# Attention and two MLPs on one core: transposes of P in float32r, row sums on DVE, PV halves joined by SBUF DMAs, and a new order of steps

## The chip, the cores and the metric

The kernel runs on one core of a Trainium2 chip. The metric is the device time of one execution in microseconds (us), as the median of the timed runs; lower is better. The engines are PE (TensorE; PEld is its loading of weights), DVE (VectorE), ACT (ScalarE), POOL (GpSimd) and SP (SyncE, which here only issues DMAs).

## The reference

Three stages follow each other. Attention takes q, k and v of shape (2, 8, 1152, 64), averages neighbouring rows of q (1152 becomes 576), and computes softmax(q k^T / 8) v. Its result, laid out as 1152 tokens by 512, goes through two MLPs.

```python
q_pool = q.reshape(B, H, S // 2, 2, D).mean(axis=3)
scores = scale * np.matmul(q_pool, k.transpose(0, 1, 3, 2))
attn = np.exp(scores - scores.max(-1)); attn /= attn.sum(-1) + 1e-9
x = heads_side_by_side(attn @ v)              # 1152 x 512
h = np.maximum(x @ w_in, 0); x = (s * h * h + b) @ w_out      # d_ff 2048
return ((x @ w_a) * (x @ w_b)) @ w_out2                       # d_ff 1536
```

## The kernel before

Matmuls run in float32r, and where more exactness is wanted an operand is split into a high and a low half (names ending in h and l): ACT makes the high half by a copy with a cast, DVE the low half by a subtraction.

Attention is worked in eight pairs of heads (NP, n from 0 to 7). A pair has nine blocks of 128 query rows (ORDER, i from 0 to 8; the block in the middle, number 4, holds the last 64 rows of both heads). The global number of a block is g = 9n + i. A block goes through these steps, each a short function that the list STEPS names:

- S01 and S2: scores on PE, 768 columns into one of two PSUM tiles and 384 into one of four shared PSUM banks (s_mm01, s_mm2). M01, M2, C: row maxima on DVE. X2, X01: exponentials on ACT into an SBUF tile E, with the row sums as a by-product, read by two small instructions.
- A: POOL adds the two row sums (s_add, L453). R: DVE takes the reciprocal (L457). N: POOL multiplies E by it (L464). E has three rooms.
- Ta, Tb, Tc: nine 128x128 transposes of E on PE, by the float32 identity, into shared banks (p_tr, L481: four, four and one). ha, hb, hc (ACT, L493) and La, Lb, Lc (DVE, L499) read each bank once and write the halves of P transposed, p2 and p3. A bank is free again when its last reader is done (bank, bank_read).
- PP: behind Tc three transposes of the next pair's k (float32r, L349) or q (float32, L369) ride in the same bank; EVh and EVl read them out.
- P0 to P3: the PV matmuls (pv_mm, L515): for each head and each of two column groups (256 and 320 columns), V against p2 or p3. V stands as high and low halves side by side, so that the 128 rows of the result are two halves that must be added.
- PVc and PVd: ACT copies the one half of 64 rows to SBUF onto the partitions of the other (pv_copy, L524), and DVE adds the other half from PSUM (pv_add, L534). XS: POOL splits the sum into xa_h and xa_l, the input of the first MLP (x_split, L95 and L98); for the last pair ACT and DVE do that.
- KS, VS, QP: POOL splits k and v and pools q, and then SP issues the load of the next pair. CV steps convert the first MLP's weights.

The order of all steps is written out by hand in SCHED, one text for one pair; a mark ' behind a name says that the step belongs to the pair before (two marks: two before), a comma to the next one. Each engine works its own part of that order strictly in sequence. MM, Fa, Fd and Fp are pieces of the first MLP that run in the last pair's order.

After attention come the first MLP (weights converted from 64-bit words along the way), the second MLP, which forms its products by sums of blocks with tiles u1, u2, u3 and u5 (u_tile, L884; copy_up and add_up write and read them), and the output.

Of the kernel before, what the change touches and what calls it, by code (L numbers as in the profile page):

```python
# [27 lines left out]
PP.8' Lb.7' Tb.8' R.0 EVh.8' hc.8' hb.8' N.0 Fp.0''''''''''''''' P2.5' M01.2 P2.6' Lc.8' S2.2 P2.7' P2.8' Ta.8'
Lb.8' M2.2 Tb.0 X01.1 C.2 A.1 R.1 S01.3 PVc.2' ha.8' PVd.2' Ta.0 La.8' hb.0 X2.2 X01.2 Tc.0 PP.0 S2.3 MM.0' N.1
Lb.0 Tc.1 M01.3 PP.1 EVh.0 A.2 M2.3 hc.0 XS.0' S01.4 ha.0 Lc.0 C.3 S2.4 R.2 EVh.1 hc.1 La.0 X2.3 CV.2 CV.3 EVl.1  # L30
N.2 X01.3 Ta.1 Lc.1 ha.1 A.3 CV.4 Tb.1 hb.1 M01.4 P3.0' P3.1' M2.4 S01.5 La.1 CV.0, C.4 R.3 P3.2' P3.3' KS.0,
CV.6' Lb.1 X2.4 Ta.2 P3.4' Tb.2 Tc.2 ha.2 P3.5' PP.2 M01.5 hb.2 P3.6' N.3 CV.5 La.2 Lb.2 CV.7' QP.0, CV.1, X01.4
CV.8''''''''''''''''''''''''''''''''''''''''''''''''''''''''''' A.4 hc.2 P3.7' S2.5 EVh.2 M2.5 P3.8' VS.1 Tb.3
Lc.2 S01.6 PVc.3' C.5 Fa.0' P0.0 PVd.3' P0.1 Fd.0' hb.3 R.4 X2.5 X01.5 P0.2 Ta.3 Lb.3 S2.6 N.4 M01.6 Tc.3 M2.6
PP.3 P0.3 ha.3 P0.4 S01.7 C.6 P0.5 EVh.3 La.3 hc.3 MM.1''''''''''''''''''''''''''''''''''''''''''''''' P0.6 Lc.3
P0.7 M01.7 X2.6 S2.7 X01.6 P0.8 A.5 XS.1' PVc.0 M2.7 Ta.4 R.5 PVd.0 C.7 ha.4 A.6 Tb.4 Tc.4 R.6 hb.4 PP.4 N.5
S01.8 La.4 Ta.5 EVh.4 N.6 hc.4 Lb.4 X2.7 Tc.5 PP.5 Lc.4 ha.5 QP.1, P1.0 P1.1 M01.8 La.5 S2.8 EVh.5 P1.2 M2.8
hc.5 X01.7 Tb.5 EVl.5 hb.5 A.7 C.8 R.7 Lc.5 P1.3
# [1077 lines left out]
```

## Time and profile before

| | |
|---|---|
| three timed runs, median (lowest to highest) | 686.64 us (686.63 to 687.0) |
| profiled execution, from its first to its last instruction | span 684.6 us, 11850 instructions |
| busy, share of the span: PE | 674.3 us, 98% |
| PEld | 647.0 us, 95% |
| DVE | 521.9 us, 76% |
| ACT | 400.3 us, 58% |
| POOL | 366.6 us, 54% |
| granted TensorE clock, mean | 1.000 |
| first attention scores to the last PV matmul | from about 8 us to 274 us |

The profile is one execution of its own. It gives no time outside of its span; the median of the timed runs is 2.0 us above the span. Matmul ends are modelled and overlap, so that the distance from one start to the next tells what a matmul costs in a row of matmuls, and its printed duration does not. The same holds, to a smaller degree, for DVE and ACT, whose next instruction often starts before the end of the one before. Idle time of an engine is put down to the one whose signal came last.

### The profile page before, as it was taken

To read this page: it belongs to the slowest core of one execution; us is meant where nothing else is said; L and a number is where in the kernel's file an instruction comes from. 1 tells how busy PE (TensorE), PEld (TensorE's weight loads), DVE (VectorE), ACT (ScalarE), POOL (GpSimd) and SP (SyncE) were. 2 spreads that over 40 slices of the span, in tenths; PEclk is the share of its full clock that TensorE was granted. 3 is DMA by queue.
4 is the path that set the end of the run, shared out by engine and by line. 5 is a ranking of instruction groups with operands and counts; after the bars stand their busy time and mean duration, and the time that the engine had idled before them with its cause. 6 is when DMAs were issued, how large, how long until landed. Compare 5 with 4: busy or idle time off the path is not lost.

```text
span 684.6 us, 11850 instructions
## 1 busy us (share of the span) xinstructions
PE 674.3 (98%) x4446; PEld 647.0 (95%) x4446; DVE 521.9 (76%) x963; ACT 400.3 (58%) x869; POOL 366.6 (54%) x374
## 2 busy tenths in 40 slices
PE   8999999999999999999999999999999999999997
PEld 7899999999999998999999999999999999998885
DVE  6999999999999996584545744879987888886431
ACT  6998999999999986454531421435433434444321
POOL 5879797979788883586535535510225442430000
PEclk9999999999999999999999999999999999999999
DMA  7121121303030010423223232250132323134004
GB/s 232 38 70 62 44 70 35 82 25 105 2 105 16 20 65 1 152 94 123 63 72 113 63 103 83 64 182 1 62 117 69 125 62 123 62 90 157 0 1 138
DMA packets 25914, 52.93 MB, mean 77 GB/s; under 512 B 1665, under 2 KB 2689, under 8 KB 25857
## 3 DMA queue, kind: packets, MB, share of 16 engines
q1 hardware_dynamic: 25776, 52.04, 23.7%
q8 instruction: 35, 0.57, 0.4%
q14 instruction: 23, 0.18, 0.1%
q10 hardware_dynamic: 80, 0.13, 0.1%
HBM read 49.81 MB, written 2.36 MB: 76 GB/s over the span
## 4 chain that ended last, share of the span: by engine, by line
PE 84%; DVE 9%; ACT 3%; POOL 2%; issue 1%; DMA 1%; SPq 0%; ACTq 0%; POOLq 0%; DVEq 0%
PE ps L630 28%; PE pp L630 17%; PE pp L950 11%; PE pv L515 9%; PE t L481 7%; PE s L404 6%; PE s L411 3%; DVE p3l L499 2%; DVE sm L430 1%; ACT p3h L493 1%; PE t L349 1%; PE t L369 1%; DVE xs L534 1%; DVE sm L427 1%; ACT x L354 1%
## 5 line engine op out<-in xcount | busy, mean ns | idle before, releaser
L481 PE MATMUL t<-ident,e 128*128 128x128 f32 x648 | 98.9, 276 | 2.3 <-POOL e L464 1.0
L464 POOL TENSOR_SCALAR e<-e,sm 128x1152 f32<-128x1152 f32 (+1 forms) x73 | 89.8, 1232 | 10.6 <-DVE sm L457 7.1
L481 PEld LDWEIGHTS t<-ident,e 128*128 128x128 f32 x648 | 75.3, 140 | 12.9 <-POOL e L464 2.3
L965 POOL TENSOR_TENSOR ab<-ab,at 128x576 f32<-128x576 f32 x24 | 35.0, 1478 | 91.0 <-ACT ab L960 87.2
L764 POOL TENSOR_SCALAR r<-r,sb_s,sb_b 128x384 f32<-128x384 f32 (+1 forms) x46 | 41.0, 902 | 57.7 <-DVE r L761 57.7
L499 DVE TENSOR_TENSOR p3l<-t,p3h 128x512 fp32r<-128x512 f32 (+1 forms) x120 | 64.2, 554 | 6.6 <-ACT p3h L493 4.2
L427 DVE TENSOR_REDUCE sm<-s 128x1 f32<-128x768 f32 x72 | 68.2, 948 | 0.1
L446 ACT ACTIVATE e<-s,sm 128x768 f32<-128x768 f32 x72 | 66.5, 923 | 0.4 <-DVE sm L435 0.4
L493 ACT CAST p3h<-t 128x512 fp32r<-128x512 f32 (+1 forms) x120 | 56.2, 485 | 5.1 <-PE t L481 2.7
L758 ACT ACTIVATE r<-ps 128x384 f32<-128x384 f32 (+1 forms) x46 | 20.1, 505 | 61.8 <-PE ps L630 61.7
L761 DVE SCALAR_TENSOR_TENSOR r<-ps,r 128x384 f32<-128x384 f32 (+1 forms) x46 | 23.8, 567 | 37.2 <-ACT r L758 37.2
L499 DVE TENSOR_TENSOR p2l<-t,p2h 128x512 fp32r<-128x512 f32 x96 | 50.8, 549 | 0.9 <-ACT p2h L493 0.7
L142 ACT ACTIVATE f<-raw 128x1024 f32<-128x1024 f32 x34 | 38.8, 1140 | 17.9 <-issue 11.1
L515 PE MATMUL pv<-p3h,v 128*128 128x320 f32 x144 | 47.6, 338 | 0.4 <-DVE p2l L499 0.4
L493 ACT CAST p2h<-t 128x512 fp32r<-128x512 f32 x96 | 45.0, 501 | 5.1 <-PE t L481 4.3
L439 ACT ACTIVATE e<-s,sm 128x384 f32<-128x384 f32 x72 | 43.0, 597 | 5.8 <-DVE sm L457 4.7
L630 PE MATMUL ps<-xa_h,wh 128*128 128x384 f32 (+1 forms) x200 | 45.3, 330 | 0.1
L146 DVE SCALAR_TENSOR_TENSOR f<-raw,f 128x1024 int32<-128x1024 int32 x34 | 44.5, 1309 | 1.1
L630 PE MATMUL ps<-xa_h,wl 128*128 128x384 f32 (+1 forms) x200 | 45.0, 328 | 0.0
L630 PE MATMUL ps<-xa_l,wh 128*128 128x384 f32 (+1 forms) x200 | 45.0, 328 | 0.0
L166 POOL TENSOR_TENSOR wl<-f,wh 128x1024 fp32r<-128x1024 f32 x16 | 40.5, 2531 | 7.1 <-ACT wh L198 5.9
L630 PE MATMUL ps<-gh,wh 128*128 128x384 f32 x192 | 43.7, 336 | 0.0
(142 smaller groups left out, 2047.1 us busy)
## 6 DMA issues: line engine op xcount, KB each, us to landing
raw<-in_moe_w_out_dram SPq DMA_DIRECT2D x14, 1024.0 KB, 5.0
raw<-in_moe_w_in_dram SPq DMA_DIRECT2D x8, 1024.0 KB, 5.7
raw<-in_moe_w_a_dram SPq DMA_DIRECT2D x6, 1024.0 KB, 5.2
raw<-in_moe_w_b_dram SPq DMA_DIRECT2D x6, 1024.0 KB, 5.1
vn<-in_v_dram SPq DMA_DIRECT2D x8, 576.0 KB, 4.0
kn<-in_k_dram SPq DMA_DIRECT2D x7, 576.0 KB, 3.9
qn<-in_q_dram SPq DMA_DIRECT2D x7, 512.0 KB, 3.8
out_dram<-ab SPq DMA_DIRECT2D x8, 256.0 KB, 2.6
```

The source lines that it names most:

```text
L146: nc.vector.scalar_tensor_tensor(out=f, in0=lo, scalar=29, in1=f, op0=ALU.logical_shift_right, op1=ALU.bitwise_or)
L404: nc.tensor.matmul(ps[:, c, 0:384], w, x[:, c * 384:(c + 1) * 384], start=(z == 0), stop=(z == len(pr) - 1))
L427: nc.vector.reduce_max(small(g)[:, 0:1], SPS[g, 0][:, :, 0:384], axis=AX.XY)
L439: nc.scalar.activation(out=e_tile(g)[:, 768:1152], in_=SPS.pop((g, 1))[:, 0:384], func=AF.Exp, bias=m[:, 2:3], accum_out=m[:, 3:4])
L446: nc.scalar.activation(out=e_tile(g)[:, 0:768].rearrange("p (a c) -> p a c", a=2), in_=SPS.pop((g, 0))[:, :, 0:384], func=AF.Exp, bias=m[: ...
L464: nc.gpsimd.tensor_scalar(out=e[:, c], in0=e[:, c], scalar1=m[:, 6:7], scalar2=1.0, op0=ALU.mult, op1=ALU.mult)
L481: nc.tensor.transpose(ps[:, i * 128:(i + 1) * 128], E[g][:, (c0 + i) * 128:(c0 + i + 1) * 128], ident)
L493: nc.scalar.copy(out=p_dst(g)[0][:, c0:c0 + n], in_=p_src(g, z))
L499: nc.vector.tensor_tensor(out=l, in0=p_src(g, z), in1=h.bitcast(F32), op=ALU.subtract)
L515: nc.tensor.matmul(ps[:, 0:N], V[n, hd][:, c].rearrange("p a d -> p (a d)"), p, start=(t == 0), stop=(t == 2 * NC - 1))
L630: nc.tensor.matmul(ps, a, c[:, o:o + n], start=(first and z == 0), stop=(last and z == 2), skip_group_check=more)
L950: nc.tensor.matmul(ps, a[x], w2_at[kf][c], start=(kf == 0 and y == 0), stop=(kf == KF2 - 1 and y == 2))
```

## The change

- E becomes one tensor of three rooms, e, and a second tensor, er, of type float32r is laid on the same bytes. The exponentials and N write by the name e. The transposes read by the name er, with the float32r identity, and write float32r into the bank. Since the two names are two tensors to the framework, three kinds of waits are written by hand: the first transpose of each group waits for N (E_DONE), and the first exponential that reuses a room waits for the transposes that read it (E_READ, e_written).
- A moves from POOL to DVE.
- For all pairs but the last, PVc copies all 128 rows of the bank, and that is the bank's only reader. PVd becomes one DMA from SBUF to SBUF, issued by SP, that moves 64 rows; for the second head a further DMA moves the other 64 rows beside the first head's. XS on POOL first adds the two tiles and then splits as before.
- A bank for a group's last transpose may be taken by the riding transposes first (t_bank), so PP may stand ahead of Tc.
- SCHED is written anew. The set of steps is the same. The block of steps that stood at the end of the text now stands at its beginning, one period later, QP.1 among them. One CV step runs four pairs earlier.
- The u tiles of the second MLP lie in the first two rooms of e instead of in a pool of their own.

```diff
--- before.py
+++ after.py
@@ -21,21 +21,21 @@
 
 
 SCHED = """
-S01.0 Ta.6' X2.8' Tb.6' Lb.5' N.7' Tc.6' PP.6' P1.4' M01.0 ha.6' hb.6' La.6' P1.5' P1.6' S2.0 EVh.6' P1.7' hc.6'
-Lb.6' X01.8' Lc.6' P1.8' M2.0 KS.1 Ta.7' EVl.6' S01.1 A.8' PVc.1' VS.0
-CV.9''''''''''''''''''''''''''''''''''''''''''''''''''''''''''''' R.8' C.0 ha.7' P2.0' PVd.1' P2.1' P2.2' X2.0
-Tc.7' La.7' PP.7' X01.0 hc.7' S2.1 Tb.7' N.8' M01.1 M2.1 A.0 C.1 EVh.7' hb.7' S01.2 Lc.7' P2.3' P2.4' X2.1 Tc.8'
-PP.8' Lb.7' Tb.8' R.0 EVh.8' hc.8' hb.8' N.0 Fp.0''''''''''''''' P2.5' M01.2 P2.6' Lc.8' S2.2 P2.7' P2.8' Ta.8'
-Lb.8' M2.2 Tb.0 X01.1 C.2 A.1 R.1 S01.3 PVc.2' ha.8' PVd.2' Ta.0 La.8' hb.0 X2.2 X01.2 Tc.0 PP.0 S2.3 MM.0' N.1
-Lb.0 Tc.1 M01.3 PP.1 EVh.0 A.2 M2.3 hc.0 XS.0' S01.4 ha.0 Lc.0 C.3 S2.4 R.2 EVh.1 hc.1 La.0 X2.3 CV.2 CV.3 EVl.1
-N.2 X01.3 Ta.1 Lc.1 ha.1 A.3 CV.4 Tb.1 hb.1 M01.4 P3.0' P3.1' M2.4 S01.5 La.1 CV.0, C.4 R.3 P3.2' P3.3' KS.0,
-CV.6' Lb.1 X2.4 Ta.2 P3.4' Tb.2 Tc.2 ha.2 P3.5' PP.2 M01.5 hb.2 P3.6' N.3 CV.5 La.2 Lb.2 CV.7' QP.0, CV.1, X01.4
-CV.8''''''''''''''''''''''''''''''''''''''''''''''''''''''''''' A.4 hc.2 P3.7' S2.5 EVh.2 M2.5 P3.8' VS.1 Tb.3
-Lc.2 S01.6 PVc.3' C.5 Fa.0' P0.0 PVd.3' P0.1 Fd.0' hb.3 R.4 X2.5 X01.5 P0.2 Ta.3 Lb.3 S2.6 N.4 M01.6 Tc.3 M2.6
-PP.3 P0.3 ha.3 P0.4 S01.7 C.6 P0.5 EVh.3 La.3 hc.3 MM.1''''''''''''''''''''''''''''''''''''''''''''''' P0.6 Lc.3
-P0.7 M01.7 X2.6 S2.7 X01.6 P0.8 A.5 XS.1' PVc.0 M2.7 Ta.4 R.5 PVd.0 C.7 ha.4 A.6 Tb.4 Tc.4 R.6 hb.4 PP.4 N.5
-S01.8 La.4 Ta.5 EVh.4 N.6 hc.4 Lb.4 X2.7 Tc.5 PP.5 Lc.4 ha.5 QP.1, P1.0 P1.1 M01.8 La.5 S2.8 EVh.5 P1.2 M2.8
-hc.5 X01.7 Tb.5 EVl.5 hb.5 A.7 C.8 R.7 Lc.5 P1.3
+M01.8' EVh.4' Lc.4' N.6' ha.5' P1.0' P1.1' P1.2' QP.1 EVh.5' La.5' EVl.5' X01.7' P1.3' hc.5' S2.8' Tb.5' M2.8' A.7'
+P1.4' S01.0 C.8' Lc.5' hb.5' X2.8' Ta.6' R.7' Lb.5' Tb.6' M01.0 ha.6' N.7' Tc.6' KS.1 PP.6' hb.6' P1.5' P1.6' La.6'
+X01.8' hc.6' Lb.6' CV.9''''''''''''''''''''''''''''''''''''''''''''''''''''''''''''' P1.7' S2.0 EVh.6' P1.8' A.8'
+Ta.7' M2.0 R.8' C.0 EVl.6' PVc.1' N.8' S01.1 Lc.6' ha.7' X2.0 X01.0 P2.0' PVd.1' P2.1' Tb.7' PP.7' Tc.7' La.7' VS.0
+S2.1 P2.2' M01.1 EVh.7' hc.7' P2.3' hb.7' S01.2 M2.1 Lc.7' C.1 Tc.8' A.0 PP.8' X2.1 Lb.7' EVh.8' P2.4' R.0
+Fp.0''''''''''''''' hc.8' M01.2 Tb.8' Lc.8' P2.5' S2.2 hb.8' Lb.8' P2.6' Ta.8' X01.1 M2.2 A.1 ha.8' N.0 C.2 P2.7' R.1
+P2.8' PVc.2' Tb.0 PVd.2' S01.3 hb.0 La.8' X2.2 Lb.0 CV.8'''''''''''''''''''''''''''''''''''''''''''''''''''''''''''
+N.1 S2.3 PP.1 M2.3 Ta.0 PP.0 X01.2 Tc.1 ha.0 M01.3 EVh.1 La.0 hc.1 Tc.0 EVh.0 C.3 KS.0, hc.0 MM.0' EVl.1 Lc.1 X2.3
+S01.4 S2.4 A.2 Ta.1 Lc.0 X01.3 Tb.1 R.2 ha.1 P3.0' M01.4 P3.1' M2.4 A.3 La.1 hb.1 Lb.1 CV.0, P3.2' S01.5 N.2 P3.3'
+Tb.2 R.3 C.4 hb.2 Ta.2 XS.0' P3.4' P3.5' ha.2 CV.3,,,, P3.6' N.3 M01.5 X2.4 Lb.2 P3.7' P3.8'
+MM.1''''''''''''''''''''''''''''''''''''''''''''''' La.2 X01.4 CV.6' CV.7' CV.2 S2.5 PP.2 Tc.2 PVc.3' CV.1, Tb.3 EVh.2
+M2.5 S01.6 P0.0 PVd.3' P0.1 hc.2 Lc.2 P0.2 S2.6 P0.3 C.5 hb.3 Lb.3 A.4 PP.3 X2.5 X01.5 Fd.0'''''' QP.0, Tc.3 Ta.3
+M01.6 EVh.3 P0.4 R.4 M2.6 hc.3 P0.5 ha.3 VS.1 Fa.0'' CV.4 S01.7 A.5 N.4 C.6 Lc.3 S2.7 R.5 X01.6 P0.6 P0.7 P0.8 La.3
+X2.6 Ta.4 M01.7 A.6 Tb.4 M2.7 PVc.0 R.6 ha.4 N.5 XS.1' CV.5 PVd.0 hb.4 Tc.4 C.7 PP.4 S01.8 La.4 X2.7 Ta.5 Lb.4 hc.4
+Tc.5 PP.5
 """.split()
 
 @with_exitstack
@@ -262,7 +262,12 @@
     ps_s01 = s01.enter_context(tc.tile_pool(name="ps_s01", bufs=2, space=PSUM))
     banks = [right(att, f"ps_{i}", 1, space=PSUM) for i in range(4)]
     v_p = right(att, "vv", 2)
-    e_p = right(att, "e", 3)
+    e_all = nc.alloc_sbuf_tensor("e", [128, 3, S], F32, side="right")
+
+
+    er_all = nc.alloc_sbuf_tensor_at("er", [128, 3, S], F32R, offset=nc.lookup_mloc(e_all).addr)
+    e_at = [e_all.ap()[:, i] for i in range(3)]
+    er_at = [er_all.ap()[:, i] for i in range(3)]
     pt_p = right(att, "pt", 1)
     xs_p = right(att, "xs", 2)
     sm_p = right(att, "sm", 4)
@@ -420,8 +425,14 @@
 
     def e_tile(g):
         if g not in E:
-            E[g] = e_p.tile([128, S], F32, tag="e", name="e")
+            E[g] = e_at[g % 3]
         return E[g]
+
+    E_DONE = {}
+
+    def e_written(g, ins):
+        for t in E_READ.pop(g - 3, ()):
+            after(ins, t, mybir.DependencyReason.ANTI)
 
     def s_max01(g):
         nc.vector.reduce_max(small(g)[:, 0:1], SPS[g, 0][:, :, 0:384], axis=AX.XY)
@@ -436,21 +447,23 @@
 
     def s_exp2(g):
         m = SM[g]
-        nc.scalar.activation(
+        ins = nc.scalar.activation(
             out=e_tile(g)[:, 768:1152], in_=SPS.pop((g, 1))[:, 0:384], func=AF.Exp, bias=m[:, 2:3], accum_out=m[:, 3:4]
         )
+        e_written(g, ins)
         bank_read(("s2", g))
 
     def s_exp01(g):
         m = SM[g]
-        nc.scalar.activation(
+        ins = nc.scalar.activation(
             out=e_tile(g)[:, 0:768].rearrange("p (a c) -> p a c", a=2), in_=SPS.pop((g, 0))[:, :, 0:384], func=AF.Exp,
             bias=m[:, 2:3], accum_out=m[:, 4:5],
         )
+        e_written(g, ins)
 
     def s_add(g):
         m = SM[g]
-        nc.gpsimd.tensor_scalar(out=m[:, 5:6], in0=m[:, 3:4], scalar1=1e-9, scalar2=m[:, 4:5], op0=ALU.add, op1=ALU.add)
+        nc.vector.tensor_scalar(out=m[:, 5:6], in0=m[:, 3:4], scalar1=1e-9, scalar2=m[:, 4:5], op0=ALU.add, op1=ALU.add)
 
     def s_rec(g):
         m = SM[g]
@@ -461,7 +474,9 @@
         e = E[g]
 
         for c in (slice(512, S), slice(0, 512)) if g == 0 else (slice(0, S),):
-            nc.gpsimd.tensor_scalar(out=e[:, c], in0=e[:, c], scalar1=m[:, 6:7], scalar2=1.0, op0=ALU.mult, op1=ALU.mult)
+            E_DONE[g, c.start] = nc.gpsimd.tensor_scalar(
+                out=e[:, c], in0=e[:, c], scalar1=m[:, 6:7], scalar2=1.0, op0=ALU.mult, op1=ALU.mult
+            )
 
     def p_dst(g):
         hd, j = ORDER[g % 9]
@@ -474,12 +489,19 @@
 
     PTC = ((0, 4), (4, 4), (8, 1))
 
+    def t_bank(g, z):
+        if (g, z) not in TP:
+            TP[g, z] = bank(("t", g, z), 2 * (g >= 0) + (rides(g) if z == 2 else 0))
+        return TP[g, z]
+
     def p_tr(g, z):
-        ps = bank(("t", g, z), 2 + (rides(g) if z == 2 else 0))
+        ps = t_bank(g, z)
         c0, n = PTC[z]
         for i in range(n):
-            nc.tensor.transpose(ps[:, i * 128:(i + 1) * 128], E[g][:, (c0 + i) * 128:(c0 + i + 1) * 128], ident)
-        TP[g, z] = ps
+            t = nc.tensor.transpose(ps[:, i * 128:(i + 1) * 128].bitcast(F32R), er_at[g % 3][:, (c0 + i) * 128:(c0 + i + 1) * 128], identr)
+            if i == 0:
+                after(t, E_DONE[g, 512 if g == 0 and z else 0], mybir.DependencyReason.DATA)
+        E_READ.setdefault(g, []).append(t)
 
     def p_src(g, z):
         c0, n = PTC[z]
@@ -499,6 +521,12 @@
         nc.vector.tensor_tensor(out=l, in0=p_src(g, z), in1=h.bitcast(F32), op=ALU.subtract)
         bank_read(("t", g, z))
 
+    SYNC = mybir.DependencyClass.Sync
+    E_READ = {}
+
+    def after(ins, earlier, why):
+        tc.add_manual_dep(ins.ins, earlier.ins.name, mybir.DependencyInfo(SYNC, why), reason="e and er are one room")
+
     TP = {}
     PV = {}
     XS = {}
@@ -507,7 +535,7 @@
         key = (n, hd, big_seg)
         N = 256 + NX if big_seg else 256
         if lo == 0:
-            PV[key] = bank(("pv", key), 2)
+            PV[key] = bank(("pv", key), 2 if n == NP - 1 else 1)
         ps = PV[key]
         for t in range(lo, hi):
             c, x = divmod(t, 2)
@@ -520,8 +548,11 @@
         ps = PV[n, hd, big_seg]
         N = 256 + NX if big_seg else 256
         a, o = (0, 64) if hd == 0 else (64, 0)
-        tmp = PVT[n, hd, big_seg] = xs_p.tile([128, 256 + NX], F32, tag="tmp", name="tmp")
-        nc.scalar.copy(out=tmp[a:a + 64, 0:N], in_=ps[o:o + 64, 0:N])
+        tmp = PVT[n, hd, big_seg] = xs_p.tile([128, 256 + NX], F32, tag=f"t{hd}", name="tmp")
+        if n == NP - 1:
+            nc.scalar.copy(out=tmp[a:a + 64, 0:N], in_=ps[o:o + 64, 0:N])
+        else:
+            nc.scalar.copy(out=tmp[:, 0:N], in_=ps[:, 0:N])
         bank_read(("pv", (n, hd, big_seg)))
 
     def pv_add(n, hd, big_seg):
@@ -529,14 +560,22 @@
         N = 256 + NX if big_seg else 256
         if (n, big_seg) not in XS:
             XS[n, big_seg] = xs_p.tile([128, 256 + NX], F32, tag="xs", name="xs")
-        xs, tmp = XS[n, big_seg], PVT.pop((n, hd, big_seg))
+        xs, tmp = XS[n, big_seg], PVT[n, hd, big_seg]
         a = 64 * hd
+        if n < NP - 1:
+
+            nc.sync.dma_start(out=xs[a:a + 64, 0:N], in_=tmp[64 - a:128 - a, 0:N])
+            if hd == 1:
+                nc.sync.dma_start(out=PVT[n, 0, big_seg][64:128, 0:N], in_=tmp[64:128, 0:N])
+            return
         nc.vector.tensor_tensor(out=xs[a:a + 64, 0:N], in0=ps[a:a + 64, 0:N], in1=tmp[a:a + 64, 0:N], op=ALU.add)
         bank_read(("pv", (n, hd, big_seg)))
 
     def x_split(n, big_seg):
         xs = XS.pop((n, big_seg))
         N = 256 + NX if big_seg else 256
+        if n < NP - 1:
+            nc.gpsimd.tensor_tensor(out=xs[:, 0:N], in0=xs[:, 0:N], in1=PVT[n, 0, big_seg][:, 0:N], op=ALU.add)
         b, hp = n // HP, n % HP
         c0 = b * SP + (256 if big_seg else 0)
         c = slice(c0, c0 + N)
@@ -565,8 +604,7 @@
     def ride(n, i):
         g = 9 * n + i
         if rides(g):
-            ps = TP[g, 2] if n >= 0 else bank(("t", g, 2), rides(g))
-            pend[n, i] = RIDES[i][2](n + RIDES[i][0], ps[:, 128:512])
+            pend[n, i] = RIDES[i][2](n + RIDES[i][0], t_bank(g, 2)[:, 128:512])
 
     def evac(n, i, z):
         if (n, i) in pend and pend[n, i][z]:
@@ -881,7 +919,8 @@
         U = {}
 
         def u_tile(name):
-            U[name] = u_p.tile([128, 2, HC], F32, tag=name, name=name)
+            i = ("u1", "u2", "u3", "u5").index(name)
+            U[name] = halves(e_at[i // 2][:, i % 2 * SP:(i % 2 + 1) * SP])
             return U[name]
 
         def copy_up(name, ps):
@@ -909,7 +948,6 @@
         ps_b.close()
         for i in range(4):
             ps2.append(ctx.enter_context(tc.tile_pool(name=f"pp{i}", bufs=1, space=PSUM, side=("right", "left")[i // 2])))
-        u_p = ctx.enter_context(tc.tile_pool(name="u", bufs=1))
         m2_p = ctx.enter_context(tc.tile_pool(name="m2", bufs=1))
         ab0 = m2_p.tile([128, 8, NT], F32, tag="ab", name="ab")
         ab1 = []
```

## Rows read from the trace of the kernel before

**Rows 1.** Busy us and instructions per engine, clock, DMA share, GB/s, three stretches.

```profile
47.82:80.14 32.32, 32.21 (x242) 31.02 (x241) 30.75 (x74) 29.82 (x80) 27.36 (x34) 1.00 0.19 56
...
240.00:260.00 20.00, 19.38 (x135) 17.68 (x133) 19.64 (x44) 17.19 (x45) 17.26 (x19) 1.00 0.17 54
...
300.00:320.00 20.00, 20.00 (x117) 20.00 (x116) 14.50 (x20) 10.34 (x20) 15.57 (x12) 1.00 0.19 65
```

**Rows 2.** Chain of waits: start us, length us, engine, tile, line.

```profile
47.82 1.43 PE s L404 x8
...
209.53 1.44 PE s L404 x8
...
268.40 3.20 PE ps L630 x24
```

**Rows 3.** Timeline of PE: start us, length us, line, out<-in, shapes.

```profile
113.76 0.33 PE L411 MATMUL s<-x,qm_h 128*128 128x384 f32 x1
...
114.46 1.04 PE L481 MATMUL t<-ident,e 128*128 128x128 f32 x8
...
115.48 0.30 PE L515 MATMUL pv<-p3l,v 128*128 128x320 f32 x1
...
115.92 0.51 PE L404 MATMUL s<-x,qh 128*128 128x384 f32 x2
...
121.56 0.28 PE L515 MATMUL pv<-p2l,v 128*128 128x256 f32 x1
121.68 0.28 PE L515 MATMUL pv<-p2h,v 128*128 128x256 f32 x1
```

**Rows 4.** Timeline of PE in narrow windows around one run of K transposes.

```profile
118.78 0.22 PE L349 MATMUL t<-identr,kc 128*128 128x128 f32 x1
...
118.90 0.25 PE L349 MATMUL t<-identr,kc 128*128 128x128 f32 x1
118.99 0.38 PE L515 MATMUL pv<-p3h,v 128*128 128x320 f32 x1
119.21 0.31 PE L515 MATMUL pv<-p3l,v 128*128 128x320 f32 x1
```

**Rows 5.** Timeline of DVE from 114.33 us on.

```profile
114.33 0.28 DVE L499 TENSOR_TENSOR p2l<-t,p2h 128x128 fp32r<-128x128 f32 x1
114.52 0.95 DVE L427 TENSOR_REDUCE sm<-s 128x1 f32<-128x768 f32 x1
115.39 0.55 DVE L430 TENSOR_REDUCE sm<-s 128x1 f32<-128x384 f32 x1
115.85 0.68 DVE L499 TENSOR_TENSOR p2l<-t,p2h 128x512 fp32r<-128x512 f32 x1
116.45 0.14 DVE L435 TENSOR_REDUCE sm<-sm 128x1 f32<-128x2 f32 x1
116.51 0.15 DVE L457 RECIPROCAL sm<-sm 128x1 f32<-128x1 f32 x1
116.58 0.67 DVE L499 TENSOR_TENSOR p2l<-t,p2h 128x512 fp32r<-128x512 f32 x1
```

**Rows 6.** Groups by line, five periods: count, busy us, mean ns, idle before.

```profile
L534 DVE TENSOR_TENSOR xs<-pv,tmp 64x320 f32<-64x320 f32 x10 | 4.8, 484 | 0.2
L534 DVE TENSOR_TENSOR xs<-pv,tmp 64x256 f32<-64x256 f32 x10 | 4.2, 422 | 0.2
```

**Rows 7.** Groups by line on POOL, the same five periods.

```profile
L453 POOL TENSOR_SCALAR sm<-sm 128x1 f32<-128x1 f32 x46 | 13.3, 289 | 15.7 <-ACT e L446 13.0
...
L98 POOL TENSOR_TENSOR xa_l<-xs,xa_h 128x320 fp32r<-128x320 f32 x5 | 4.4, 875 | 0.4
```

**Rows 8.** DMA issues of the page: count, KB each, us to landing.

```profile
raw<-in_moe_w_in_dram SPq DMA_DIRECT2D x8, 1024.0 KB, 5.7
...
qm<-in_q_dram SPq DMA_DIRECT2D x16, 32.0 KB, 3.2
```

## The prediction

> **What bounds the kernel now.** I read the busy time per stretch first, then the chain of waits, then the timeline of TensorE by starts, and the other engines after it. In a stretch of attention PE is busy 32.21 of 32.32 us, but DVE 30.75 and ACT 29.82 are close, and in the MLP stretch (300 to 320) PE is busy 20.00 of 20 with DVE at 14.50 [rows 1]. The chain names the same score matmul once per pair of heads, six times from 47.82 to 209.53: a period of 32.33 us [rows 2]. From 268.40 on it runs through the first MLP's matmuls, where PE has no idle time. So whatever attention saves should stand at the end.
>
> A busy PE is no proof that PE is the limit, so I count one period by starts. Scores: 8 blocks of 6 matmuls and one of 12 make 60, at (114.46 - 113.76)/4 = 0.175 us: 10.5. PV: 36 of 320 columns at (115.92 - 115.48)/3 = 0.147 and 36 of 256 at 0.12: 9.6. A run of 8 float32 transposes takes 115.48 - 114.46 - 0.147 = 0.873, its after-effect on the next matmul included: 0.109 each; 81 of P and 9 of q make 9.8 [rows 3]. The K transposes are float32r already: three start at 118.78, (118.84) and 118.90, PV follows at 118.99 and its second matmul at 119.21 instead of 0.147 later, so a run of three costs 0.283, and six make 1.7 [rows 4]. Sum 31.6 of 32.33. PE is the limit, with 0.7 lost.
>
> DVE by starts: M01 0.87, M2 0.46, C 0.06, R 0.07 for each of 9 blocks; 18 large L at 0.60, 9 small at 0.19; q's lower halves 1.5 (estimate from the same steps); four PV adds, some 1.6 by their durations less overlap [rows 5, 6]. Sum 13.1 + 10.8 + 1.7 + 1.5 + 1.6 = 28.7 to 29.2; I use 29.0. That is 5 to 6% under its busy time, because ends overlap. ACT's 29.82, less the same share, is an estimate of 28.2.
>
> **The transposes of P.** In float32r they have the K transposes' form (same shapes, same engine). Within a run the step is 0.06; the run's last one costs 0.09, and the next matmul is 0.075 late: 0.1 per run on top. The new order has 15 runs in a period; in two of them q's float32 transposes come last. So 99 x 0.062 = 6.1, plus 13 x 0.1 = 1.3, plus q's 1.0, is 8.4 against 11.5 now: 3.1 less. PE would need 28.5. Bounds per transpose: 0.06 below, and above the 0.109 of now. The nearest rows, K's, decide for 0.06.
>
> The longest float32r run now is three [rows 4]. The Trainium skill (TensorE: Matmul & The Clock Gate, "Back-to-back issue gap") gives about 81 ns for a matmul of 128 columns in a stream where each loads its weights, more than these starts show; by its figure 99 transposes would take 8.0 instead of 6.1, 1.9 us more per period. No row shows a long run, so this is a rival below.
>
> **The row sums on DVE.** POOL loses 9 x 0.289 = 2.6 per period, and its waits for the exponential (13.0 in five periods) go to DVE [rows 7]. No row shows this operation on DVE; the nearest is R, 0.07 by starts and 0.157 by duration at most: 0.6 to 1.4, I take 0.7. The handing from POOL to R goes. Each now waits on DVE for X01's accumulator; behind it stand L (which frees the bank that PE's next transposes want), M01 and M2. In the new order an A stands beside C or behind M2, and the next L behind it waits for an ACT copy that itself stands behind that X01 (A.0, Lb.7' and X01.0, hb.7'). So a wait there mostly replaces one that L would have. Cost taken: nothing; the cover is ACT's order; if it goes, up to 2.6 per period.
>
> **The PV halves.** DVE loses four adds: 1.6. The ACT copies keep their columns and take 128 partitions: nothing below, and above 0.07 each (384 columns on 128 partitions against 320 on 64, an estimate); I take nothing. POOL gets an add per half, like xa_l, 0.875 and about 0.74: 1.6. So POOL loses 1.0 net. SP issues six DMAs per period, in order with the q, k and v loads. Those have much room: a load of one pair serves the next. Small transfers land 3.2 us after issue, the largest 5.7 [rows 8]. XS on POOL waits for them, and the next N is queued behind it, then Ta. Between PVd.2' and XS.0' POOL has N.1, KS.0 and N.2, about 4.5 us; between PVd.3' and XS.1' it has VS.1, N.4 and N.5. I take 3.2 as landing, so nothing; at 5.7, 1.2 per XS. A PV bank is free one reader earlier: a gain that I don't count (0 to 0.3).
>
> **The new order and the rooms.** E still has three rooms, and X2 still waits for the transposes of three blocks before; a transpose still waits for N. Running QP.1 a period later still leaves PP.6 behind it. One conversion step (ACT) moves from the last pair to the fourth: 1.1 us of ACT elsewhere. The u tiles in E's room keep writer, reader and order, under a PE that is 20.00 of 20 busy: nothing; without that cover a copy's wait. What the reordering itself does no row can tell; it is in the share lost.
>
> **The sum.** After: PE 28.5, DVE 29.0 - 1.6 + 0.7 = 28.1, ACT 28.2, POOL below its 27.4. Two bounds for the period: PE keeps its share lost now (0.7 of 31.6), 29.2; or DVE keeps its own (29.0 of 32.33 used), 31.3. PE sets the period now, so I stay nearer to the first, but three engines within 0.4 us of each other leave less cover: 29.7, a gain of 2.6. Six such periods (the pairs between the first and the last) give 15.6. Before the first of them PE waits for loads and for DVE: 0 to 2.5, I take 0.8. In the last pair (240 to 260: PE 19.38, DVE 19.64 [rows 1]) DVE limits as much as PE, and the pair keeps its old adds: 0 to 2.5, I take 1.5. Together 17.9. The span is 684.6 and the median 2.0 above it; I take the gain off both: span 666.7, time 668.7.
>
> **Rivals.**
> - DVE and ACT take over: period 31.3. 6 x 1.0 + 0.9 at the ends = 6.9: 679.7. For it: their busy shares are 95% and 92% already. Against: some of their idle time now is waiting for PE.
> - Long float32r runs don't keep 0.06: at the run-of-three mean, 0.094, 99 cost 9.3 and with q 10.3, 1.2 less than now: period 31.1, time 678. For it: no long run in any row; against: the step inside K's runs is even. The skill's 81 ns lies between.
> - Nearly everything is had: period 29.0, ends 3.5: 663.
> - The change doesn't do what it says: P's transposes keep 0.109 under the other name; PE still needs 31.6, and only the 0.7 lost can shrink: 685. Against: K's rows.
> - Slower: the waits for the exponential come to DVE in full. The period of the first rival, 31.3, plus 2.6 is 33.9, 1.6 more than now, six times: 696. It decides from 1.0 us of such waits per period on top of that rival. For it: POOL waits so now, 21 times in five periods; against: the order around A.
>
> **How the numbers follow.** Forecast 0.50 (its own range 665 to 673); DVE and ACT 0.17; long runs 0.10; nearly everything 0.10; not what it says 0.04; slower 0.09. The range 663 to 681 leaves out the slower case, the one that doesn't do what it says, and half of the fastest: 0.18. 0.2% is 1.4 us, about what a measurement tells from no change. Faster: 0.50 + 0.17 + 0.10 + 0.10 + 0.01 = 0.88; within: 0.03 + 0.02 = 0.05; slower 0.07.
>
> **What would show it.** Right: starts of P's transposes 0.06 apart, the score matmul of the chain every 29 to 30.5 us, DVE idle before A near nothing, the first MLP matmul near 250, the clock still 1.00. Wrong, step by step: steps of 0.08 or more inside long runs; a period above 31 with DVE or ACT nearly full; DVE idle, released by ACT at A; POOL idle, released by the new DMAs at XS; idle PE in the MLP, which would give the gain back.

## The result and the profile after

The changed kernel takes 678.56 us as a median (678.51 to 680.6) against 686.64: the ratio is 0.989 (interval 0.9876 to 0.9904). The forecast was 668.7. The direction was right and the range held it, but the gain is 8.1 us where 17.9 were forecast. The profiled execution has a span of 676.7 (684.6 before) and took 678.51; its mean granted clock is 0.999.

The windows of the changed kernel (window, then its length and the busy time of PE, PEld, DVE, ACT and POOL with the number of instructions, the granted clock, the DMA share, GB/s): an ordinary pair, the fourth pair, and the stretch of the first MLP that [rows 1] has too.

```profile
65.17:95.97 30.80, 30.78 (x242) 29.64 (x240) 29.38 (x79) 28.92 (x78) 26.33 (x27) 1.00 0.26 73
95.97:127.82 31.85, 30.93 (x242) 29.65 (x240) 29.38 (x78) 29.98 (x79) 26.29 (x27) 1.00 0.26 71
300.00:320.00 20.00, 20.00 (x117) 20.00 (x117) 7.37 (x11) 7.61 (x16) 11.16 (x9) 1.00 0.32 106
```

PE is still busy in 30.78 of 30.80, now in a period of 30.80 instead of 32.32; DVE is down from 30.75 to 29.38 and ACT from 29.82 to 28.92. The fourth pair is 1.05 longer than the third, and there PE is idle for 0.9. The chain of waits again names the score matmul (start, length, work); it answers to [rows 2]:

```profile
46.20 1.57 PE s L409 x8
76.97 1.58 PE s L409 x8
107.77 1.57 PE s L409 x8
139.61 1.61 PE s L409 x8
170.42 1.63 PE s L409 x8
```

The distances are 30.77, 30.80, 31.84 and 30.81: an ordinary pair gains 1.54 where 2.6 were forecast. Through the whole of an ordinary pair the chain stays on PE (shares of that pair, by line):

```profile
by line: PE pv L543 32.6%; PE s L409 24.2%; PE t L501 23.3%; PE s L416 12.1%; PE t L354 4.6%; PE t L374 3.3%; issue 0.1%
```

So in the changed kernel, as it stands, PE is the limit of an ordinary pair. By the first row maxima of each pair on DVE, the whole span comes apart like this:

| stretch | before | after | gain | forecast |
|---|---|---|---|---|
| up to the second pair | 35.07 | 34.40 | 0.67 | 0.8 |
| four ordinary pairs (2, 3, 5 and 6), each | 32.34 | 30.80 | 1.54 | 2.6 |
| fourth pair | 32.32 | 31.85 | 0.47 | 2.6 |
| seventh pair | 32.68 | 32.10 | 0.58 | 2.6 |
| last pair, to the first MLP matmul | 38.72 | 38.22 | 0.50 | 1.5 |
| from there to the end | 416.48 | 416.95 | -0.47 | 0 |

The gains add up to 7.9, the change of the span. Missing are 4 x 1.06 = 4.2 in the ordinary pairs, 2.1 and 2.0 in the fourth and seventh, 1.1 at the two ends of attention and 0.5 behind it.

The timeline of PE shows the form of transposes whose price the forecast took from [rows 4] (start, time, line, work, count of rows alike):

```profile
79.09 0.81 PE L501 MATMUL t<-identr,er 128*128 128x128 f32 x8
79.73 0.38 PE L543 MATMUL pv<-p3h,v 128*128 128x320 f32 x1
79.95 0.30 PE L543 MATMUL pv<-p3l,v 128*128 128x320 f32 x1
```

From the first start to the next matmul's are 0.64, and that matmul takes 0.22 to the next start instead of the usual 0.147. The run of eight so costs 0.64 + 0.075 = 0.71; the same run took 0.873 before [rows 3], and the forecast had 8 x 0.062 + 0.1 = 0.60. Counted by starts as in the prediction, PE's own work in an ordinary pair is 29.88 (31.54 before, 28.5 forecast) and 0.92 is lost (0.79 before, 1.2 forecast). These sums depend on what each start is taken to cost, and are good to some 0.2. The runs with P's transposes take 9.7 by these prices, not 8.4.

### The profile page after: what moved, and what is told of

The parts are those of the page before. It is cut to its first block, busy times and chain, and to the rows that moved or that the text cites. A ratio compares the mean times of both kernels' runs of the same rounds, so it can differ in the third digit from the quotient of the medians.

```text
span 676.7 us, 12040 instructions
## 1 busy us (share of the span) xinstructions
PE 664.4 (98%) x4446; PEld 637.3 (94%) x4446; DVE 513.9 (76%) x1007; ACT 394.3 (58%) x869; POOL 356.1 (53%) x316
## 4 chain that ended last, share of the span: by engine, by line
PE 88%; DVE 6%; ACT 2%; POOL 1%; issue 1%; DMA 1%; SPq 0%; DVEq 0%; POOLq 0%
PE ps L668 29%; PE pp L668 17%; PE pp L988 11%; PE pv L543 10%; PE s L409 7%; PE t L501 7%; PE s L416 4%; PE t L354 1%; PE t L374 1%; DMA tmp<-tmp 1%; DVE sm L438 1%; PE warm L685 1%; POOL e L477 1%; DVE e L930 1%; DVE f L146 1%
## 5 line engine op out<-in xcount | busy, mean ns | idle before, releaser
L501 PE MATMUL t<-identr,er 128*128 128x128 f32 x648 | 77.1, 246 | 2.7 <-POOL e L477 1.4
L501 PEld LDWEIGHTS t<-identr,er 128*128 128x128 f32 x648 | 65.7, 140 | 11.3 <-POOL e L477 2.2
L515 ACT CAST p3h<-t 128x512 fp32r<-128x512 f32 (+1 forms) x120 | 55.2, 501 | 11.5 <-PE t L501 10.7
L521 DVE TENSOR_TENSOR p2l<-t,p2h 128x512 fp32r<-128x512 f32 (+1 forms) x96 | 51.3, 550 | 2.1 <-ACT p2h L515 1.6
L515 ACT CAST p2h<-t 128x512 fp32r<-128x512 f32 (+1 forms) x96 | 46.8, 518 | 3.6 <-PE t L501 1.9
L543 PE MATMUL pv<-p3h,v 128*128 128x320 f32 x144 | 45.9, 329 | 0.0
L668 PE MATMUL ps<-gh,wl 128*128 128x384 f32 x192 | 43.7, 336 | 0.0
```

The lines of the kernel that those rows point to most:

```text
L501: t = nc.tensor.transpose(ps[:, i * 128:(i + 1) * 128].bitcast(F32R), er_at[g % 3][:, (c0 + i) * 128:(c0 + i + 1) * 128], identr)
L515: nc.scalar.copy(out=p_dst(g)[0][:, c0:c0 + n], in_=p_src(g, z))
L521: nc.vector.tensor_tensor(out=l, in0=p_src(g, z), in1=h.bitcast(F32), op=ALU.subtract)
L543: nc.tensor.matmul(ps[:, 0:N], V[n, hd][:, c].rearrange("p a d -> p (a d)"), p, start=(t == 0), stop=(t == 2 * NC - 1))
L668: nc.tensor.matmul(ps, a, c[:, o:o + n], start=(first and z == 0), stop=(last and z == 2), skip_group_check=more)
```

## The experiments

Two theories stand against each other. The first: PE is the limit, its work came out larger because long float32r runs are dearer than K's runs of three, and what is taken off PE comes off the period. The second: another engine, or the written order, holds the period near 30.6, whatever PE needs. Edits are to the changed kernel where nothing else is said.

**m1_runs: the price of a run by itself.** A kernel of its own sets runs of 1 to 16 between matmuls of 320 columns whose operands are all there.

```python
for kind in ("f32", "f32r", "plain"):       # two kinds of transposes; plain float32r matmul
    for n in (1, 2, 3, 4, 6, 8, 12, 16):
        for _ in range(4): filler(4); run(kind, n)
```

> A kernel of its own, not the reference's computation: runs of 1 to 16 transposes (float32, float32r) and of plain float32r matmuls of the same shape stand between 320-column matmuls, with nothing to wait for. Theory 1 (the step of a long float32r run is a price of the operation): steps of 0.06, 0.06 and then 0.085 us from the third on, 0.075 after-effect on the next matmul, so a run of 8 costs about 0.70 and one of 16 about 1.39; float32 0.109 flat; plain matmuls like float32r transposes, if it is the loading of weights. Theory 2 (the longer steps in the changed kernel are waiting for E or for banks): 0.06 all through, a run of 16 costs about 1.06.

The timeline of PE, for each run its row and the filler behind it; L94 is float32, L96 float32r:

```profile
56.07 1.91 PE L94 MATMUL t<-ident,e 128*128 128x128 f32 x16
57.73 0.39 PE L88 MATMUL pv<-p3h,v 128*128 128x320 f32 x1
...
59.81 0.22 PE L96 MATMUL t<-identr,er 128*128 128x128 f32 x1
59.87 0.80 PE L88 MATMUL pv<-p3h,v 128*128 128x320 f32 x4
...
64.33 0.38 PE L96 MATMUL t<-identr,er 128*128 128x128 f32 x3
64.54 0.38 PE L88 MATMUL pv<-p3h,v 128*128 128x320 f32 x1
...
76.11 0.80 PE L96 MATMUL t<-identr,er 128*128 128x128 f32 x8
76.75 0.38 PE L88 MATMUL pv<-p3h,v 128*128 128x320 f32 x1
...
87.84 1.49 PE L96 MATMUL t<-identr,er 128*128 128x128 f32 x16
89.17 0.38 PE L88 MATMUL pv<-p3h,v 128*128 128x320 f32 x1
```

From the run's start to the filler's: 0.06 for one, 0.21 for three, 0.64 for eight, 1.33 for sixteen. From 8 to 16 that is 0.69 / 8 = 0.086 each, and from 3 to 8 0.43 / 5 = 0.086. So the first two cost 0.06 each and all later ones 0.085, with nothing to wait for, and the run of eight repeats that of the kernel to 0.01. Sixteen float32 transposes take 1.66 to the filler's start; with the 0.08 by which the filler's own step is longer (0.23 instead of 0.147) that is 0.109 each. The first theory's price is shown. K's runs of three could not show it: only their last step is a later one. Plain float32r matmuls were expected to cost what the float32r transposes do; they cost more (last section).

**e1_f32_transposes: the whole change, but P's transposes in float32.**

```diff
-  nc.tensor.transpose(ps[...].bitcast(F32R), er_at[g % 3][...], identr)
+  nc.tensor.transpose(ps[...], E[g][...], ident)
```

> The changed kernel with P's transposes in float32 again (by the name e, with the float32 identity), all else as changed. Theory 1 (PE still sets the period, and what was won is the transposes' price): transposes cost 11.5 instead of 9.7 us a period, so PE needs 31.6, period 32.3, time 687 to 690: nothing is left of the gain. Rival (the other parts, row sums, PV halves and order, carry half of the gain or more): below 683.

686.4 us, ratio 0.9999 (0.999 to 1.0009). Window of an ordinary pair:

```profile
67.34:99.31 31.97, 31.97 (x243) 31.08 (x241) 29.62 (x79) 29.26 (x78) 26.27 (x27) 1.00 0.25 71
```

The time is a little under the expected 687. PE has no idle time at all, and the other parts of the change together are worth nothing in the whole while it has this much to do (an ordinary pair gains 0.37, the fourth loses 0.68). So PE was the limit, as forecast.

**e2_f32r_alone: the kernel before, with P's transposes in float32r under the second name.** Of the rest of the change it has only the new place of the u tiles.

```diff
+ er_all = nc.alloc_sbuf_tensor_at("er", [128, 3, S], F32R, offset=...)   # and the waits
- nc.tensor.transpose(ps[...], E[g][...], ident)
+ nc.tensor.transpose(ps[...].bitcast(F32R), er_at[g % 3][...], identr)
```

> The kernel before with float32r transposes of P alone (e, er and the u tiles as changed); its order of steps, row sums on POOL and PV adds on DVE. Theory 1: the 15 to 18 runs of the old order cost 9.8 instead of 11.5, PE needs 29.9, DVE 29.0 to 29.2 by starts: period 30.7 to 31.2, 676 to 680, nearly the whole gain. Rival (row sums, PV halves and order are needed for it): 683 to 686, because DVE and ACT are not relieved.

684.57, ratio 0.9972 (0.9962 to 0.9983): 2 us, less than the first theory gave and inside the rival's 683 to 686.

```profile
66.98:99.13 32.15, 31.29 (x243) 29.57 (x241) 30.62 (x74) 29.77 (x78) 27.41 (x34) 1.00 0.19 57
```

PE's work is 29.99 by starts, 1.5 less than before, but 2.16 are lost now instead of 0.79. PE was freed and the old order had no use for it: the chain of waits through this pair now lies on POOL, where A still stands, for 12 of its 32 us. With e1: the transposes, and the rest of the change, are each worth 0 to 2 us alone and 8 together.

**e3_less_pe: 2.16 us per pair less on PE,** by leaving out the matmuls of p2 with the low half of the one column group.

```diff
+ if x and not big_seg:
+     continue
```

> The changed kernel without the PV matmuls of p2's low half (18 of 256 columns a period, 2.16 us of PE, left out). Theory 1 (PE sets the period at 29.8 and 1.0 lost; next is DVE at 29.5 by starts): the period falls by 0.6 to 1.1 to 29.7 to 30.2, time 671 to 674, and no further. Theory 2 (DVE and ACT with their waits hold the period already): 30.8 stays, 678. If only PE mattered: 28.7, 664.

676.56, ratio 0.9856 (0.984 to 0.9872), where the first theory gave 671 to 674. Here it fails:

```profile
64.39:95.02 30.63, 30.00 (x224) 27.45 (x222) 29.28 (x79) 28.80 (x78) 26.24 (x27) 1.00 0.27 74
```

PE has 29.88 - 2.16 = 27.72 by starts to do, less than the forecast's 28.5, and the period falls by 0.17 only, to 30.63. The chain of waits, which stayed on PE in the changed kernel, now leaves it for 8.0 us of this pair and lies on ACT; in some of the other pairs DVE, or POOL, carries a further part (start, length, work):

```profile
81.04 0.31 PE t L501 x4
...
81.37 0.38 ACT p3h L515
...
88.77 0.57 ACT e L450 x2
...
89.38 0.63 PE t L501 x5
```

In that stretch ACT has no idle time, and in the same part of a pair of the changed kernel it is only 0.07 short of that (windows of e3, then of the changed kernel):

```profile
81.37:89.38 8.01, 7.69 (x57) 6.82 (x55) 6.91 (x18) 8.01 (x22) 7.13 (x7) 1.00 0.32 86
```

```profile
82.40:90.40 8.00, 8.00 (x65) 7.83 (x64) 6.90 (x19) 7.93 (x22) 7.12 (x8) 1.00 0.34 95
```

So behind PE's path stands one over ACT that is shorter by 0.17 at most. If time taken off the transposes does no more than time taken off the PV matmuls, 29.7 was out of reach even had the transposes kept 0.062.

**e4_no_row_sum and e5_less_pe_dve: is DVE the floor?** e4 leaves A out (R takes the one row sum alone), which frees 9 x 0.121 = 1.09 of DVE; e5 is e3 and e4 together.

```diff
- nc.vector.tensor_scalar(out=m[:, 5:6], in0=m[:, 3:4], ...)
- nc.vector.reciprocal(m[:, 6:7], m[:, 5:6])
+ nc.vector.reciprocal(m[:, 6:7], m[:, 4:5])
```

> The changed kernel without the row sum A (R takes the reciprocal of X01's part alone; the rest of the sum is left out): DVE loses 9 x 0.121 = 1.09 us a period, PE nothing. Theory 1 (PE sets the period of 30.8: 29.9 by starts and 0.9 lost): it stays at 30.6 to 30.8, time 677.5 to 678.7. Theory 2 (DVE sets it): 29.8, time 671 to 673.

> Both at once: without the PV matmuls of p2's low half (PE 2.16 us less a period) and without the row sum A (DVE 1.09 less). With PE alone relieved the period stayed at 30.62. Theory 1 (the floor behind PE is DVE's work in its order): the period falls by about 0.9 to 1.1, to 29.5 to 29.7, time 669 to 671. Rival (the floor is ACT's order, or the one stretch in which ACT waits 1.3 us for the transposes behind P3): 30.3 to 30.6, 674.5 to 676.5.

e4 takes 678.39 (ratio 0.9878, 0.9861 to 0.9894) with a period of 30.8 to 30.9, the same as the changed kernel: while PE has its 29.9, DVE sets nothing. e5 takes 676.44 (0.9847, 0.9832 to 0.9862), inside the 674.5 to 676.5 that its rival, ACT's order, gave; its ordinary pairs take 30.58 as a mean, against e3's 30.63. So neither PE's sum nor DVE's is the floor. The same stretch in e5, and in e12, which follows:

```profile
82.00:90.00 8.00, 7.75 (x57) 6.88 (x57) 6.72 (x16) 8.00 (x23) 7.26 (x7) 1.00 0.32 86
```

```profile
80.40:88.40 8.00, 7.83 (x61) 7.14 (x60) 6.96 (x17) 8.00 (x21) 7.36 (x8) 1.00 0.35 96
```

ACT fills it without a gap in both (8.00 of 8.00), while DVE idles for 1.0 to 1.3. ACT's sum over the whole pair, 28.8 of 30.6 in e3, does not show that.

**e12_less_all: e5, and 0.8 us per pair less on ACT,** by not reading the row sum of X2 (`accum_out` left out there).

> Without p2's low PV matmuls (PE 2.16 us less), without A (DVE 1.09 less), and also without the reading of X2's row sum (ACT 9 x 0.09 = 0.8 less a period). Theory 1 (behind PE the period is a chain that runs on DVE in one stretch and on ACT in another, so that relief counts only for its part of the chain): 30.56 falls by 0.2 to 0.5, 673 to 675. Rival (ACT alone is the floor): by 0.8, 670 to 671. If nothing moves: the floor is the order of PE and POOL.

672.85, ratio 0.9796 (0.9781 to 0.9811), a period of 30.09 by the median of the ordinary pairs, 0.46 less than e5's 30.56. The 0.8 taken from ACT gave 0.46, the 2.16 taken from PE 0.17. This is what a chain that runs over ACT for a part of the period should do; three of the nine readings left out, some 0.1 each, stand in the stretch shown above. It is not the whole of it: in three of its five pairs from the second to the sixth the chain lies on DVE for some 10 us and on POOL for 2.5, and on ACT for 3 to 4 only. Several paths are nearly tied there. The time came out slightly below the expected band.

**e7_moved: the two short stretches beside the ordinary pairs.** In the changed kernel a conversion step of 1.17 us stands on ACT in the fourth pair, and the last PE wait is in the MLP. The timelines of ACT and PE there (the bracket is the idle time before, and what ended it):

```profile
113.91 1.17 ACT L142 ACTIVATE f<-raw 128x1024 f32<-128x1024 f32 x1
...
115.69 0.45 PE L416 MATMUL s<-x,qh 128*128 128x384 f32 x1 [0.90 <-ACT e L450]
...
272.75 0.53 PE L668 MATMUL ps<-xa_h,wh 128*128 128x288 f32 x2 [0.59 <-DVE r L799]
```

```diff
- ... ha.2 CV.3,,,, P3.6' ...         ... Fd.0'''''' ...   ... Fa.0'' ...
+ ... Lb.1 CV.3,,,, CV.0, P3.2' ...   CV.6' CV.7' Fa.0' Fd.0' ...
```

> The changed kernel with three steps moved: the first weight conversion on ACT (CV.3, fourth pair) ahead of hb.2, where ACT waits 1.33 us for the transposes anyway, and the first MLP's Fa and Fd ahead of PVc.3'. Theory 1 (CV.3 at its place delays PE by 1.05 in one pair; Fa and Fd late cost 0.59 of PE idle in the MLP): 1.0 to 1.6 less than the changed kernel's 678.5, so 676.9 to 677.5. Rival (both are absorbed elsewhere): 678.5.

676.66, ratio 0.9853 (0.9837 to 0.987): 1.9 less than the changed kernel, a little more than expected. The fourth pair:

```profile
95.99:126.79 30.80, 30.78 (x242) 29.66 (x240) 29.38 (x78) 30.02 (x79) 26.35 (x27) 1.00 0.27 74
```

ACT has the same step in it (30.02 against 29.98) and the pair takes 30.80 instead of 31.85. So the place of the step cost 1.05, not its length. The gap in the MLP is gone as well, and its length is 416.10.

**e11_tb2_early: e7 with Tb.2 two steps earlier, ahead of S01.5,** to test whether the chain can be shortened there.

> As the kernel with three steps moved, and in each period Tb.2 stands ahead of S01.5, where ACT waits 1.33 us for it. Theory 1 (PE sets the period; splitting a run of eight transposes costs it 0.1): 0 to 1 more than that kernel. Rival (that wait holds the period through ACT and DVE): 0.3 less per period, 2 less in all.

681.16, ratio 0.992 (0.9906 to 0.9935); the period is 31.39, 0.6 longer, which neither expectation gave. The trace has the place where it is lost:

```profile
80.28 1.23 POOL L477 TENSOR_SCALAR e<-e,sm 128x1152 f32<-128x1152 f32 x1 [0.24 <-DVE sm L470]
81.48 0.72 POOL L578 TENSOR_TENSOR xs<-xs,tmp 128x256 f32<-128x256 f32 x1
...
82.29 0.51 PE L501 MATMUL t<-identr,er 128*128 128x128 f32 x4 [0.48 <-POOL xs L578]
```

PE now comes to the four transposes of Tb.2 too early and idles until POOL has done N.2 and the add of XS behind it. Such a wait comes once in each of seven pairs, 3.6 us in all of the 4.5 by which e11 is slower than e7; in e7 PE waits for nothing in an ordinary pair. That one of the two POOL steps alone holds the transposes is not shown.

**e6_old_order and e6b_load_behind: the changed instructions in the order of before.** e6 takes SCHED from the kernel before and leaves the rest of the change.

> The changed kernel in the old order of steps (float32r transposes, row sums on DVE and PV halves by DMA stay). PE by starts needs about 30.0 in that order too. Theory 1 (the new order is needed: in the old one DVE meets A where it has to wait for ACT, and PE loses 2.2 as with float32r alone): period 31.6 to 32.2, 683 to 687. Rival (the parts alone relieve DVE enough): 30.8 to 31.2, 678 to 681.

715.44, ratio 1.0415 (1.04 to 1.0431), far above what either theory gave. ACT's, SP's, POOL's and PE's timelines in one pair:

```profile
92.85 0.43 ACT L555 COPY tmp<-pv 128x320 f32<-128x320 f32 x1
...
95.13 0.37 SPq L325 DMA_DIRECT2D vn<-in_v_dram  x1
95.60 0.46 SPq L567 DMA_DIRECT2D xs<-tmp  x1
...
100.18 0.86 POOL L578 TENSOR_TENSOR xs<-xs,tmp 128x320 f32<-128x320 f32 x1 [3.87 <-DMA xs<-tmp]
...
103.79 0.87 PE L501 MATMUL t<-identr,er 128*128 128x128 f32 x5 [3.88 <-POOL e L477]
```

The old order issues the next pair's v load (576 KB) right ahead of the transfers of the PV halves. That load may not start before POOL has read the buffer that it fills (VS.1, done at 95.10), and SP worked its issues in order. So the halves, copied by 93.28, are issued 2.3 us late, at 95.60, and land 4.2 and 3.9 later (the change's median is 2.1). POOL's add waits 3.87 for them, N is queued behind the add, and PE waits 3.88 for N. This is the prediction's own row of waits, DMA to XS to N to Ta. e6b issues the v load behind XS.1 and keeps the rest of e6.

```diff
- VS=then_load(v_split, load_v), ... XS=x_split
+ VS=v_then_load, ... XS=x_then_load     # load_v(n + 2) behind XS.1; VS loads only pair 1's v
```

> The changed kernel in the old order of steps, as before (715), but with the load of the next pair's v issued behind XS.1 instead of ahead of PVd.3's DMAs. Theory 1 (the old order costs so much because the PV halves queue behind the 576 KB load of v, POOL waits for them at XS.1 for 3.9 us, and N, the transposes and the clock suffer from it): that wait goes, the period falls from 37.2 to 32 to 33, time 683 to 690. Rival (A's place on DVE in the old order is what costs): 36 to 37 stays, 705 to 715.

686.31, ratio 0.9999 (0.9987 to 1.001); pairs of 31.7 to 33.0. POOL's waits at the add in a pair fall (total, times, longest; e6, then e6b):

```profile
POOL xs L578 <- DMA xs<-tmp: 4.6, 2, 3.9
```

```profile
POOL xs L578 <- DMA xs<-tmp: 1.8, 2, 1.1
```

One moved load gave 29 us back. In e6b the halves are issued as soon as they are copied (88.14 and 88.17) and land 3.8 and 3.4 later: most of what it gave is the earlier issue, not the shorter landing. What is left, 686.31 against 678.56, is the new order's share, in which the add waits once in the whole run, in the seventh pair:

```profile
211.04 0.37 SPq L134 DMA_DIRECT2D raw<-in_moe_w_in_dram  x1
211.50 0.47 SPq L567 DMA_DIRECT2D xs<-tmp  x1
...
218.32 0.88 POOL L578 TENSOR_TENSOR xs<-xs,tmp 128x320 f32<-128x320 f32 x1 [2.31 <-DMA tmp<-tmp]
...
221.97 0.96 PE L501 MATMUL t<-identr,er 128*128 128x128 f32 x9 [0.62 <-POOL e L477]
223.62 0.33 PE L374 MATMUL t<-ident,qpm 128*128 128x128 f32 x1 [0.57 <-POOL qpm L330]
```

It is e6's pattern again: a 1024 KB weight load, held until DVE's conversion step has read its buffer (until 211.01), stands ahead of the halves, which were copied by 209.38. They land 6.5 and 6.2 after their issue. POOL is late from there on, and PE waits for it twice about the start of the last pair, 1.2 us together. No run moved this load, so what it costs the whole kernel is not shown.

**e8_sum_on_pool: the new order, with A on POOL as before.**

```diff
- nc.vector.tensor_scalar(out=m[:, 5:6], in0=m[:, 3:4], ...)
+ nc.gpsimd.tensor_scalar(out=m[:, 5:6], in0=m[:, 3:4], ...)
```

> The changed kernel with A on POOL again, at its new place in the order. DVE loses 1.09 us a period, POOL gains 9 x 0.37 = 3.4 on 26.3 and waits at A for ACT again. Theory 1 (PE sets the period; what DVE is spared is worth nothing, and N comes later): 30.9 to 31.8, 679 to 685. Rival (DVE sets the period): below 676.

720.12, ratio 1.0485 (1.047 to 1.0501), much slower than expected. The waits of one pair of 35.77 us:

```profile
DVE sm L470 <- POOL sm L466: 3.6, 5, 1.8
POOL sm L466 <- ACT e L458: 2.7, 2, 2.2
```

POOL waits for the exponential, and R waits on DVE for POOL. On DVE, in the changed kernel, no wait at A shows in any ordinary pair; in the old order (e6 and e6b) DVE waits there 0.7 once in the pair looked at. So the order and the place of A belong together.

## Why the prediction was right and wrong

**The step that failed** is the price of P's transposes: "99 x 0.062 = 6.1, plus 13 x 0.1 = 1.3, plus q's 1.0, is 8.4 against 11.5 now". From the third on a step is 0.085. That makes 9.7, and PE's work 29.88 instead of 28.5: 1.3 of the 1.4 that PE has too much. "The nearest rows, K's, decide for 0.06" was the mistake: runs of three were taken as the price for runs of 4 to 12. The rival for it, 0.094 each, gave 31.1 and 678; measured are 30.80 and 678.56. It had a chance of 0.10. That its time is so near is partly luck: the ordinary pairs gained more than it gave, the fourth and seventh less. The Trainium skill's "Back-to-back issue gap" (TensorE: Matmul & The Clock Gate), about 81 ns in a stream, agrees with the 0.085 of the later steps and not with the 0.06 of the first two.

**A second step was wrong as well,** and by e3 would have failed even with the right price: "PE sets the period now, so I stay nearer to the first ... 29.7". It adds up each engine over the whole pair and lets the largest sum, plus a small loss, be the period. e3 has 27.72 on PE and still 30.63: there the chain lies on ACT for 8.0 us in which ACT is full, before and behind it on PE. A path that changes engine can be longer than any one engine's sum. In the changed kernel PE's path is the longer one, so the dear transposes are what its period shows; but by 0.17 at most, so cheaper ones would soon have met the next path, as e3 did. The bounds of 29.2 to 31.3 did hold.

**The conversion step** at "1.1 us of ACT elsewhere", with no cost, cost 1.05 in the fourth pair (e7). In the seventh, two conversion steps stand on DVE (0.69 and 2.04; before, the second of them stood in the last pair); DVE is busy for 31.62 of 32.10 and PE only for 31.31, with a wait of 0.52 for DVE behind the longer of them; the gain is 0.58. No run changed that alone. In the MLP the 0.59 gap at 272.75 is new and went with e7's Fa and Fd; the forecast had nothing there.

**The row sums on DVE:** 0.121 each by starts, 1.1 per pair where 0.7 was taken, inside 0.6 to 1.4. The 13.0 of waits that POOL had did not come to DVE, as argued. e8 shows what A costs on POOL at its new place. The slower rival's condition, 1.0 per period of such waits on DVE, was not met even in the old order, where 0.7 shows in a pair; what made e6 slow was the transfer.

**The PV halves:** landing has a median of 2.1 and at most 6.5 (3.2 and 5.7 were the rows); XS waits nothing in an ordinary pair, as forecast. The cover named, work between PVd and XS, was not the whole of it: e6, and the seventh pair of the changed kernel, show that what stands ahead of the transfer on SP's queue matters more. "I take 3.2 as landing, so nothing" left out that SP may be held by a load.

**The ends:** 0.67 at the start (0.8 forecast), 0.50 in the last pair (1.5 forecast), where PE waits the 1.2 for the late POOL, and 0.47 lost in the MLP. The u tiles cost nothing that shows, and the clock stayed at 1.00.

**Still open:** which of the nearly tied paths holds 30.1 once PE, DVE and ACT are all relieved, and what the seventh pair's late transfer and its conversion steps cost, each by itself. The PV halves added the old way within the new order were not tried.

## What to carry to other kernels

Price a repeated operation from runs as long as the ones it will stand in, or measure it by itself first: two steps of a run of three said 0.06, and the third on is 0.085. A freed engine shortens a hand-written order only as far as the next path behind the chain; look at which engine is full in each stretch of the period, not at sums per period. Before a small transfer is put on a path that something waits for, look what is issued ahead of it on its queue, and what that waits for.

## What the runs showed of the hardware

- Float32r transposes of 128x128 start 0.06, 0.06 and then 0.085 apart, and the matmul behind them costs 0.075 more (m1_runs and the changed kernel). Float32 transposes have one even price, 0.109, in runs of 1 to 16: the last one's step is 0.03 and the matmul behind it costs 0.08 more. Plain float32r matmuls of the same 128 columns (m1_runs) are dearer than either: 0.06 for the first step, then 0.112 each, and 0.05 on the matmul behind.
- SP issued its DMAs in the order written: in e6 the transfers of the PV halves, ready at 93.28, were issued at 95.60 behind a load that waited for its buffer until 95.10.
- In e6, PE's granted clock fell after the idle stretch of 3.9 us (windows, columns as above):

```profile
95.00:99.90 4.90, 4.90 (x40) 4.56 (x38) 4.69 (x14) 4.47 (x14) 1.31 (x2) 1.00 0.58 161
99.90:103.70 3.80, 0.01 (x1) 0.00 (x0) 1.55 (x3) 0.78 (x4) 3.35 (x4) 0.74 0.04 8
103.70:107.00 3.30, 3.21 (x15) 3.21 (x16) 0.69 (x1) 2.13 (x5) 2.91 (x4) 0.50 0.00 0
107.00:110.00 3.00, 3.00 (x23) 2.92 (x22) 2.71 (x8) 1.43 (x4) 1.41 (x2) 0.74 0.53 197
110.00:113.00 3.00, 3.00 (x24) 2.97 (x23) 3.00 (x9) 3.00 (x10) 2.49 (x3) 1.00 0.00 0
```

  PE ran its 15 matmuls of the third window at 0.50, the lower level of 1.2 GHz, and came back to 1.00 in the last. The longer wait so cost more than itself: PE waits 2.8 more here than in e6b's pair (3.9 against 1.1), and the pair takes 37.16, 4.5 more than e6b's 32.66.
